# Attention forward and backward: queries repeated through DRAM, and o and dQ of a block taken from PSUM by one operation

## The chip, the cores and the metric

One core of one Trainium2 chip. The metric is the device time of one execution, in microseconds (us); for a set of runs the median is given. The engines are TensorE (PE, with its weight loads as PEld), VectorE (DVE), ScalarE (ACT) and GpSimd (POOL). SyncE (SP) issues DMAs and computes nothing. Each engine executes its instructions strictly in the order in which they were put into its queue.

## What is computed

The reference is the forward pass of two attention branches and its vector-Jacobian product with `grad_out`; it returns the joined output [1, 2048, 896] and the eight gradients (of both inputs and all weights). S = 2048, D = 448, 16 heads of 28 columns, bf16. Branch A is linear attention. Branch B, which the change touches, is softmax attention in which 16 query heads share one key head and one value head:

```python
q = (x @ wq).reshape(B, S, H, Dh).transpose(0, 2, 1, 3)
k = x @ wk
v = x @ wv
scores = jnp.einsum("bhqd,bkd->bhqk", q, k) * (Dh ** -0.5)
p = softmax(scores)
o = jnp.einsum("bhqk,bkd->bhqd", p, v)
return o.transpose(0, 2, 1, 3).reshape(B, S, H * Dh) @ wo
...
_out, _vjp = jax.vjp(_f, A_x, A_wqkv, A_wo, B_x, B_wq, B_wk, B_wv, B_wo)
_grads = _vjp(grad_out)
return (_out, *_grads)
```

## The kernel before

The program has three parts. Branch A, forward and backward, and the preparation of branch B take some 207 us. The main loop (L922) does the softmax attention forward and backward together, up to about 1000 us. A last part multiplies the gradients of queries, keys and values with weights and inputs.

**Units and blocks.** The loop runs `for u in range(NU + 28)`, NU = 512. A block b (64 of them, `blk(b)`) is 256 queries (`qc`, 8 of these) of two heads (`pair`); the 16 heads lie in four groups of four (g = pair // 2), 32 rows each, so that a block occupies 64 of a group's 128 rows (hp = pair % 2). A unit is two 128-row tiles of keys for the two heads of one block; eight units make a block. "u≡5" below is a unit with u mod 8 = 5. Everything inside the loop stands under `manual_schedule`: the order of each engine's queue is the order of the code.

**What one unit u issues.** PE multiplies queries and keys to scores S of unit u into two of three PSUM banks SB, and do and values to the gradient D of unit w = u − 16 into two banks DB (`rows_SD`, all recorded under L676). ACT exponentiates half 0 (L955) into eT, copies half 1 of D to SBUF (cp, L971) and exponentiates half 1 (L997): three activations of 128x512 a unit. DVE multiplies half 0 of D by eT into dsT (L967); POOL does half 1 from cp (L972). DVE then transposes dsT of unit u − 18 in 32x32 pieces into dsx (L1041). On even units PE accumulates `o_dq`: o of the units u − 2, u − 1 (from eT) in rows 0 to 63 of one PSUM bank `oq`, and dQ of the units u − 20, u − 19 (from dsT) in rows 64 to 127. On odd units it accumulates dK (`dk_m`) from dsx and qX, beginning with block b at u = 8b + 27.

**Once in four units** SP issues a DMA transpose of eT into eN (L999), which PE uses for dV 20 units after the block began.

**Once per block**, in this order: u≡1, DVE copies o from `oq` to the f32 tile oTs, rows 0 to 63 (L983); u≡2, PE transposes it into the spare SB bank (L809), DVE copies that back into oTs (L817), POOL multiplies it with do (L821), then the reciprocal of the row sums and two more POOL products (L830, L831); u≡3, DVE scales dQ of the block 19 units back out of `oq`, rows 64 to 127, into qT_B, over the queries of that block (L986); u≡4, `row_D`, a DVE sum (L835) and two short POOL products (L836, L837); u≡6, PE transposes the normalised gradient (L845) into the spare bank and DVE copies it to doT (L852). The spare bank is the bank into which the next unit's scores go, so that copy stands before them. `due(u, lag)` returns the block b for which u = 8b + lag.

**The queries for dK** lie in qX in another layout: four copies of each 32-row head piece, one for each quarter of the rows. For each `qc` and group, POOL copies the queries four times over into the one staging tile qst, in two operations of 128x512 (`qc_copy`, L856), and SP transposes it into qX (`qc_T`, L860, 128x1024). In every 64 units this is done in the units with u mod 64 = 29, 30, 37, 38, 45, 46, 53, 54, for the next 256 queries. The first 256 queries are done ahead of the loop by POOL and DVE. qX has two buffers, one for even and one for odd `qc`, each [128, 4, 2, 512].

**Beside these**, the attention's output products go to DRAM: from u = 144 a part of a row tile every 8 units, with a DVE copy (L747) and for each row tile one store on POOL's DMA queue (L749, 112 KB).

Of the kernel before, what the change touches and what calls it, by code (L numbers as in the profile page):

```python
# [9 lines left out]
ALU = mybir.AluOpType  # L10
AX = mybir.AxisListType
BF16 = mybir.dt.bfloat16
# [5 lines left out]
P = 128  # L18
# [7 lines left out]
def kernel(  # L26
# [624 lines left out]
    with ExitStack() as cs_:  # L651
        pe_ = cs_.enter_context(tc.tile_pool(name="ceT", bufs=1, side="right"))
        pn_ = cs_.enter_context(tc.tile_pool(name="ceN", bufs=1, side="right"))
        pd_ = cs_.enter_context(tc.tile_pool(name="cdsT", bufs=5, side="right"))
        pqa_ = cs_.enter_context(tc.tile_pool(name="cqXa", bufs=1, side="right"))
        px_ = cs_.enter_context(tc.tile_pool(name="cdsx", bufs=2, side="right"))
        pqb_ = cs_.enter_context(tc.tile_pool(name="cqXb", bufs=1, side="right"))
# [48 lines left out]

        woTp, gbT = R4, R2.rearrange("p t (c k) -> p t c k", k=P)

        qst = pp_.tile([P, 8, 4, 32], BF16, name="qst", bufs=1)[:, :, :, :]
        identF = pp_.tile([P, P], F32, name="identF", bufs=1)  # L710
        make_identity(nc, identF[:])
        oTs = pp_.tile([P, 256], F32, name="oTs", bufs=1)
        wo = pc_.tile([P, 4, D], BF16, name="wo", bufs=1)
        oTq = flat(R4).rearrange("p (t k) -> p t k", k=P)
        W4 = D // 4
# [97 lines left out]
        def o_copy(b):  # L813
            qc, pair, g, hp = blk(b)
            onp = onps.pop(b)
            os_ = oTs[:, 0:P].rearrange("p (q h c) -> p q h c", q=2, h=2)
# [34 lines left out]
            doT[b] = pw_.tile([P, 256], BF16, name="doT", bufs=2)  # L851
            nc.vector.tensor_copy(out=doT[b][r:r + 64, :], in_=tps2.pop(b)[r:r + 64, 0:256])  # L852

        def qc_copy(eng, st, qc, g, s):
            src = qT_B[g][:, qc * 256:(qc + 1) * 256].rearrange("p (b j s) -> p b j s", b=4, s=2)[:, :, :, s]
            eng.tensor_copy(out=st.rearrange("p (b s) a j -> p b s a j", s=2)[:, :, s, :, :],  # L856
                            in_=src.unsqueeze(2).to_broadcast([P, 4, 4, 32]))

        def qc_T(st, qc, g):
            nc.sync.dma_start_transpose(qX[qc].rearrange("p b s c -> p (b s) c")[:, :, g * P:(g + 1) * P],  # L860
                                        st.rearrange("p n a j -> p (n a j)"))

        dk_two = SB[2]

        def dk_m(b, m, other=0):
            qc, pair, g, hp = blk(b)
            h, B, s = m // 8, (m // 2) % 4, m % 2
            for a in range(4):
                rhs = dsx[b][32 * a:32 * a + 32, :, h, :, :].rearrange(
                    "p u t (b i s) -> p u t b i s", b=4, s=2)[:, :, :, B, :, s]  # L870
                k = 32 * ((a + 2) % 4) if other else 32 * a
                mmt((dk_two if other else dk_acc)[k:k + 32, :],
                    qX[qc][32 * a:32 * a + 32, B, s, pair * 64 + 32 * h:pair * 64 + 32 * h + 32],
                    rhs, (32 * a, k), other == 2 or b == 0 and m == 0, other == 0 and b == NB - 1 and m == 15)

        def o_mm(v):
            b, tp = divmod(v, 8)
# [43 lines left out]
        do_slots.update({32 + 8 * n: (13 + n // 4, n % 4 * P, n % 4 * P + P) for n in range(12)})  # L921
        with tc.manual_schedule():  # L922
            nc.sync.dma_start(wo, wo_d[:, 0:D].rearrange("(g p) c -> p g c", p=P))
            qX[0] = pqa_.tile([P, 4, 2, 512], BF16, name="qX")
            for g in range(4):
                st = pd_.tile([P, 2, 512], BF16, name="dsT").rearrange("p a (n j) -> p a n j", j=32).rearrange(
                    "p a (n b) j -> p (a n) b j", b=4)
                qc_copy(nc.gpsimd, st, 0, g, 0)
                qc_copy(nc.vector, st, 0, g, 1)
                qc_T(st, 0, g)  # L930
            for u in range(NU + 28):
                w = u - 16
                hasS = u < NU
# [29 lines left out]
                if hasD:  # L963
                    dst = pd_.tile([P, 2, 512], BF16, name="dsT")
                    dsT[w] = dst
                    ew = eT(w)
                    nc.vector.tensor_tensor(out=dst[:, 0, :], in0=dp[0][:, :], in1=ew[:, 0, :], op=ALU.mult)  # L967
                    if (b := due(u, 12)) is not None:
# [3 lines left out]
                    nc.gpsimd.tensor_tensor(out=dst[:, 1, :], in0=cp[:, :], in1=ew[:, 1, :], op=ALU.mult)  # L972
                gq, iq = divmod(u % 64 - 29, 8)
                qq = u // 64 + 1
                if 0 <= gq < 4 and u < 448:
                    if gq == 0 and iq == 0:
                        qX[qq] = (pqb_ if qq % 2 else pqa_).tile([P, 4, 2, 512], BF16, name="qX")
                    if iq < 2:
                        qc_copy(nc.gpsimd, qst, qq, gq, iq)
                if u == 7:  # L980
                    nc.vector.memset(oTs[64:128, :], 0.0)
# [14 lines left out]
                if hasS:  # L996
                    nc.scalar.activation(out=eT(u)[:, 1, :], in_=sp[1][:, :], func=ACT.Exp, scale=scale)  # L997
                    if u % 4 == 3:
                        nc.sync.dma_start_transpose(ENs[u // 4 % 6][:, :, :],  # L999
                                                    ETs[u // 4 % 5][:, :, :, :].rearrange("p a b c -> p (a b c)"))  # L1000
                    if 0 <= gq < 4 and iq == 1 and u < 448:
                        qc_T(qst, qq, gq)
# [157 lines left out]
```

## Time and profile before

| | |
|---|---|
| three runs | 1046.53, 1037.56, 1041.17 us; median 1041.17 |
| the profiled execution | 1044.09 us |
| its span | 1042.4 us, granted TensorE clock 1.0 |
| busy: PE, DVE, ACT, POOL | 1003.5 (96%), 886.9 (85%), 865.2 (83%), 812.3 (78%) us |
| L972, POOL product, 128x512 | x512, 584.6 us, 1156 ns each |
| L1041, DVE transpose, 128x512 f32 | x512, 356.7 us, 697 ns each |
| L967, DVE product, 128x512 | x512, 340.3 us, 665 ns each |
| L955, L997, L971, ACT, 128x512 | x512 each, 325.5, 333.4, 327.0 us |
| L856, POOL copy of queries, 128x512 | x56, 34.2 us, 611 ns each |
| L983, DVE o copy; L986, DVE dQ; 64x256 | x64 each, 405 and 427 ns |
| L852, DVE doT copy, 64x256 | x64, 288 ns |

How to read it: instructions on ACT and DVE overlap at their ends (ACT's activations last 0.64 us and start 0.48 us apart), so a sum of durations exceeds what an engine's time line holds; the busy time of a stretch counts covered time once. A row names the engine, the line, the operation, output <- input by the program's names, and the tile. "x4" after a time-line row means that four such instructions in a row were drawn as one. The DMA share is the mean over the 16 DMA engines that all queues use; packets in several queues count several times, so it can exceed 1.

### The profile page before, as it was taken

Reading aid. Unit: us, or ns where it says so; the run is one execution under the profiler, and the core shown is the slowest. Engines: PE = TensorE matmul, PEld = TensorE weight load, DVE = VectorE, ACT = ScalarE, POOL = GpSimd, SP = SyncE. Lnnn points to the kernel's source line nnn. Section 1 sums busy time; section 2 is a strip of 40 time slices with the busy share of each in tenths; the row PEclk is TensorE's granted clock in tenths of the full one; section 3 lists DMA queues with packets and bytes.
Section 4 is the critical chain, followed back from the end, with each engine's and each line's share of the span. In section 5 each row is a group of like instructions: output and inputs, shape, how many; then the busy total and the mean of one; then the engine's idle time right before and its main releaser. Section 6 shows DMA issues by size and latency. Waiting matters only on the chain.

```text
span 1042.4 us, 40109 instructions
## 1 busy us (share of the span) xinstructions
PE 1003.5 (96%) x16245; PEld 485.1 (47%) x16245; DVE 886.9 (85%) x1780; ACT 865.2 (83%) x1743; POOL 812.3 (78%) x1106
## 2 busy tenths in 40 slices
PE   9999999999999999999999999999999999999998
PEld 5555554434444444444444444444444444444444
DVE  7897500669999999999999999999999999999942
ACT  6463132599999999999999999999999999999632
POOL 8601282238998998999999989998999999889860
PEclk9999999999999999999999999999999999999999
DMA  9879999299999999999999999999999999999983
GB/s 261 157 137 191 176 229 218 38 161 201 194 187 192 187 193 194 202 187 194 201 193 195 192 187 204 198 182 202 188 197 186 195 195 195 200 188 203 228 168 90
DMA packets 689058, 195.15 MB, mean 187 GB/s; under 512 B 670408, under 2 KB 686688, under 8 KB 688872
## 3 DMA queue, kind: packets, MB, share of 16 engines
q1 hardware_dynamic: 680392, 179.97, 105.0%
q0 software_dynamic: 4544, 9.46, 3.0%
q10 hardware_dynamic: 3936, 3.16, 1.0%
q8 instruction: 127, 2.08, 0.8%
q14 instruction: 59, 0.48, 0.2%
HBM read 12.60 MB, written 10.84 MB: 22 GB/s over the span
## 4 chain that ended last, share of the span: by engine, by line
PE 39%; DVE 25%; POOL 16%; ACT 8%; issue 7%; DMA 3%; DVEq 0%; SPq 0%; ACTq 0%; POOLq 0%
PE agen L81 13%; POOL dsT L972 12%; DVE dsT L967 10%; PE agen L676 9%; DVE dsx L1041 9%; PE aacc L676 8%; PE aacc L81 7%; ACT cp L971 4%; ACT eT L997 2%; DMA eN<-eT 2%; DVE doT L852 1%; DVE R L986 1%; POOL qst L856 1%; POOL prod L821 1%; PE aacc L809 1%
## 5 line engine op out<-in xcount | busy, mean ns | idle before, releaser
L972 POOL TENSOR_TENSOR dsT<-cp,eT 128x512 bf16<-128x512 bf16 x512 | 584.6, 1156 | 49.4 <-ACT cp L971 42.6
L1041 DVE STREAM_TRANSPOSE dsx<-dsT 128x512 f32<-128x512 f32 x512 | 356.7, 697 | 5.8 <-POOL dsT L972 3.2
L676 PEld LDWEIGHTS <-R 32*128 32x128 bf16 (+1 forms) x9104 | 245.1, 94 | 243.3 <-issue 192.5
L967 DVE TENSOR_TENSOR dsT<-agen,eT 128x512 bf16<-128x512 f32 x512 | 340.3, 665 | 11.3 <-PE agen L676 5.4
L971 ACT ACTIVATE cp<-agen 128x512 bf16<-128x512 f32 x512 | 327.0, 639 | 11.8 <-PE agen L676 9.7
L955 ACT ACTIVATE eT<-aacc 128x512 bf16<-128x512 f32 x512 | 325.5, 636 | 12.0 <-PE agen L676 6.8
L997 ACT ACTIVATE eT<-aacc 128x512 bf16<-128x512 f32 x512 | 333.4, 651 | 0.0
L676 PE MATMUL agen<-dsx,qX 32*32 32x512 bf16 x4024 | 264.0, 376 | 0.0
L676 PE MATMUL agen<-doT,R 32*128 32x256 bf16 x2048 | 243.5, 269 | 4.1 <-DVE dsT L967 3.2
L676 PE MATMUL aacc<-R,R 32*128 32x256 bf16 (+1 forms) x2240 | 207.9, 267 | 16.7 <-DVE doT L852 6.6
L676 PE MATMUL agen<-dsT,R 128*32 128x256 bf16 x2048 | 155.5, 273 | 0.5 <-issue 0.5
L676 PE MATMUL agen<-eT,R 128*32 128x256 bf16 x2048 | 155.5, 273 | 0.1
L676 PEld LDWEIGHTS <-qX 32*32 32x32 bf16 x4096 | 78.3, 89 | 112.5 <-issue 54.1
L676 PE MATMUL aacc<-eN,don 128*32 128x512 bf16 x1024 | 91.7, 387 | 1.0 <-DMA eN<-eT 1.0
L81 PEld LDWEIGHTS <-R 128*128 128x128 bf16 x517 | 40.9, 98 | 41.0 <-issue 10.6
L81 PE MATMUL agen<-R,R 128*128 128x448 bf16 (+1 forms) x180 | 42.1, 361 | 0.3 <-DVE pq L244 0.3
L676 PEld LDWEIGHTS <-don 128*32 128x32 bf16 x1024 | 21.1, 93 | 42.5 <-issue 42.5
L856 POOL COPY qst<-R 128x512 bf16<-128x512 bf16 x56 | 34.2, 611 | 5.0 <-DVE dsx L1041 2.5
L821 POOL TENSOR_TENSOR prod<-R,oTs 128x128 f32<-128x128 bf16 x64 | 27.5, 430 | 9.0 <-DVE oTs L817 9.0
L586 DVE TENSOR_TENSOR osb<-R 32x512 bf16<-32x512 bf16 x4 | 1.7, 413 | 35.4 <-DMA R<-xa 33.8
L427 POOL COPY pk<-R 128x256 bf16<-128x256 bf16 x4 | 1.6, 399 | 37.7 <-DVE R L389 37.7
L262 POOL TENSOR_SCALAR wdq<-wdq 128x448 bf16<-128x448 bf16 x16 | 21.1, 1326 | 12.0 <-DVE phiT L243 12.0
(235 smaller groups left out, 1000.1 us busy)
## 6 DMA issues: line engine op xcount, KB each, us to landing
eN<-eT SPq DMA_TRANSPOSE x128
xa<-in_A_x_dram SPq DMA_DIRECT2D x8, 224.0 KB
ga<-in_grad_out_dram SPq DMA_DIRECT2D x4, 448.0 KB
out_dram<-osb ACTq DMA_DIRECT2D x16, 112.0 KB
xa<-in_grad_out_dram POOLq DMA_DIRECT2D x4, 448.0 KB, 7.1
out_dram<-wdq POOLq DMA_DIRECT2D x8, 224.0 KB, 5.5
eT<-in_grad_out_dram SPq DMA_DIRECT2D x4, 448.0 KB
eT<-in_B_x_dram SPq DMA_DIRECT2D x4, 448.0 KB
```

The costliest lines, as they stand in the source:

```text
L81: nc.tensor.matmul(out_ap, lhsT=lhsT, rhs=rhs, start=start, stop=stop, tile_position=(0, 0))
L262: nc.gpsimd.tensor_scalar(out=wq_n[:, st, 0:D], in0=wq_n[:, st, 0:D], scalar1=1.0, scalar2=None, op0=ALU.min)
L676: nc.tensor.matmul(out, lhsT=lhsT, rhs=rhs, start=start, stop=stop, tile_position=pos, skip_group_check=True)
L809: nc.tensor.transpose(onp[:, qb, :, :].rearrange("p h c -> p (h c)"), oTs[0:64, qb * P:(qb + 1) * P], identF[0:64, 0:64], tile_position=(0 ...
L821: nc.gpsimd.tensor_tensor(out=prod[b][:], in0=dnv, in1=os_, op=ALU.mult)
L856: eng.tensor_copy(out=st.rearrange("p (b s) a j -> p b s a j", s=2)[:, :, s, :, :], in_=src.unsqueeze(2).to_broadcast([P, 4, 4, 32]))
L955: nc.scalar.activation(out=eT(u)[:, 0, :], in_=sp[0][:, :], func=ACT.Exp, scale=scale)
L967: nc.vector.tensor_tensor(out=dst[:, 0, :], in0=dp[0][:, :], in1=ew[:, 0, :], op=ALU.mult)
L971: nc.scalar.activation(out=cp[:, :], in_=dp[1][:, :], func=ACT.Copy)
L972: nc.gpsimd.tensor_tensor(out=dst[:, 1, :], in0=cp[:, :], in1=ew[:, 1, :], op=ALU.mult)
L997: nc.scalar.activation(out=eT(u)[:, 1, :], in_=sp[1][:, :], func=ACT.Exp, scale=scale)
L1041: nc.vector.transpose(out=dsx[b][:, tp, :, :, :].rearrange("p h t c -> p (h t c)").bitcast(F32), in_=dsT[y][:, :, :].rearrange("p h c -> p ...
```

## The change

1. **Queries.** They are handled by group G of two blocks (32 groups of 16 units) and not by 256 queries of all groups. At u = 16G + 5 POOL makes one copy of 128x256 in another order of columns (`q_split`) and SP transposes it into a tile qtr. At u = 16G + 14 a DMA on POOL's queue writes qtr to DRAM four times (`q_out`, 512 rows of 512 bytes). At u = 16G + 20 another DMA on POOL's queue reads it back into qX (`q_in`, 128 rows of 2 KB), for `dk_m` from u = 16G + 27. qX is a pool of two buffers of [128, 4, 2, 128]. The 56 POOL copies and 28 transposes in the loop go, and so do the four POOL copies, four DVE copies and four transposes ahead of it.
2. **dQ.** Its products come 6 units later: units u − 26, u − 25 at an even u. From u = 514 on the rest is caught up, four units at a time. The pool of dsT grows from 5 to 11 buffers.
3. **o and dQ.** At u≡1 one DVE operation takes all 128 rows of `oq`, o of block b and dQ of block b − 3, into oTs, times a column that holds 1 in rows 0 to 63 and the scale in the others. At u≡5 DVE copies dQ from oTs to qT_B (SBUF to SBUF, f32 to bf16, 64x256). The first three o and the last three dQ are taken alone. The transposed o (L817) goes to a tile of its own, osu.
4. `row_D` of block 0, which was left out because no D is issued in that unit, runs at u = 12, and the memset of oTs is replaced by two of the scale column.

```diff
-        pd_ = ... tc.tile_pool(name="cdsT", bufs=5, side="right")
-        pqa_ = ... tc.tile_pool(name="cqXa", bufs=1, side="right")
-        pqb_ = ... tc.tile_pool(name="cqXb", bufs=1, side="right")
+        pd_ = ... tc.tile_pool(name="cdsT", bufs=11, side="right")
+        pq_ = ... tc.tile_pool(name="cqX", bufs=2, side="right")
...
-        qst = pp_.tile([P, 8, 4, 32], BF16, name="qst", bufs=1)[:, :, :, :]
+        qst = pp_.tile([P, 2, 32, 4], BF16, name="qst", bufs=1)[:, :, :, :]
+        qtr = pp_.tile([P, 2, P], BF16, name="qtr", bufs=1)[:, :, :]
+        q_d = [dpool.tile([512, 256], BF16, name=f"q_d{i}") for i in range(32)]
...
+        osu = pp_.tile([P, P], F32, name="osu", bufs=1)
+        o_dq_scale = pp_.tile([P, 1], F32, name="odqs", bufs=1)
+        dqs = {u: (u - 26, u - 25) for u in range(0, NU + 1, 2)}
+        dqs.update({NU + 2 + 2 * n: tuple(range(488 + 4 * n, 492 + 4 * n)) for n in range(4)})
+        dqs.update({NU + 12 + 2 * n: (504 + 2 * n, 505 + 2 * n) for n in range(4)})
...
-        def qc_copy(eng, st, qc, g, s):
-            src = qT_B[g][:, qc * 256:(qc + 1) * 256].rearrange("p (b j s) -> p b j s", b=4, s=2)[:, :, :, s]
-            eng.tensor_copy(out=st.rearrange("p (b s) a j -> p b s a j", s=2)[:, :, s, :, :],
-                            in_=src.unsqueeze(2).to_broadcast([P, 4, 4, 32]))
-
-        def qc_T(st, qc, g):
-            nc.sync.dma_start_transpose(qX[qc].rearrange("p b s c -> p (b s) c")[:, :, g * P:(g + 1) * P],
-                                        st.rearrange("p n a j -> p (n a j)"))
+        def q_split(G):
+            qc, g = divmod(G, 4)
+            src = qT_B[g][:, qc * 256:(qc + 1) * 256].rearrange("p (b j s) -> p s j b", b=4, s=2)
+            nc.gpsimd.tensor_copy(out=qst, in_=src)
+            nc.sync.dma_start_transpose(qtr, qst.rearrange("p s j b -> p (s j b)"))
+
+        def q_out(G):
+            nc.gpsimd.dma_start(q_d[G].rearrange("(a p) c -> p a c", a=4),
+                                qtr.rearrange("p s c -> p (s c)").unsqueeze(1).to_broadcast([P, 4, 256]))
+
+        def q_in(G):
+            qX[G] = pq_.tile([P, 4, 2, P], BF16, name="qX")
+            nc.gpsimd.dma_start(qX[G].rearrange("p b s c -> p (b s c)"), q_d[G].rearrange("(p b) c -> p (b c)", b=4))
...
+        def dq_to(b):
+            qc, pair, g, hp = blk(b)
+            return qT_B[g][64 * hp:64 * hp + 64, qc * 256:(qc + 1) * 256]
...
-                if 0 <= gq < 4 and u < 448:
-                    if gq == 0 and iq == 0:
-                        qX[qq] = (pqb_ if qq % 2 else pqa_).tile([P, 4, 2, 512], BF16, name="qX")
-                    if iq < 2:
-                        qc_copy(nc.gpsimd, qst, qq, gq, iq)
+                if u == 12:
+                    row_D(0)
+                if hasS and u % 16 == 5:
+                    q_split(u // 16)
+                if hasS and u % 16 == 14:
+                    q_out(u // 16)
+                if 0 <= u - 20 < NU and u % 16 == 4:
+                    q_in(u // 16 - 1)
...
                 if (b := due(u, 9)) is not None:
-                    nc.vector.tensor_copy(out=oTs[0:64, :], in_=oq[0:64, 0:256])
-                if (b := due(u, 27)) is not None:
-                    qc, pair, g, hp = blk(b)
-                    nc.vector.tensor_scalar(out=qT_B[g][64 * hp:64 * hp + 64, qc * 256:(qc + 1) * 256],
-                                            in0=oq[64:128, 0:256], scalar1=scale, scalar2=None, op0=ALU.mult)
+                    if b < 3:
+                        nc.vector.tensor_copy(out=oTs[0:64, :], in_=oq[0:64, 0:256])
+                    else:
+                        nc.vector.tensor_scalar(out=oTs[:, :], in0=oq[:, 0:256], scalar1=o_dq_scale[:, 0:1], scalar2=None,
+                                                op0=ALU.mult)
+                if (b := due(u, 37)) is not None and b < 61:
+                    nc.vector.tensor_copy(out=dq_to(b), in_=oTs[64:128, :])
...
                 else:
-                    o_dq((u - 2, u - 1), (u - 20, u - 19))
+                    ys = dqs.get(u, ())
+                    o_dq((u - 2, u - 1), ys[:2])
+                    o_dq((-1, -1), ys[2:])
```

The new copy at u≡5 is called "the cast L999" in the prediction, after its line in the changed kernel.

More of the change, by code (lines that the diff above doesn't have):

```diff
@@ L653 @@
         pn_ = cs_.enter_context(tc.tile_pool(name="ceN", bufs=1, side="right"))
-        pd_ = cs_.enter_context(tc.tile_pool(name="cdsT", bufs=5, side="right"))
-        pqa_ = cs_.enter_context(tc.tile_pool(name="cqXa", bufs=1, side="right"))
+        pd_ = cs_.enter_context(tc.tile_pool(name="cdsT", bufs=11, side="right"))
+        pq_ = cs_.enter_context(tc.tile_pool(name="cqX", bufs=2, side="right"))
         px_ = cs_.enter_context(tc.tile_pool(name="cdsx", bufs=2, side="right"))
-        pqb_ = cs_.enter_context(tc.tile_pool(name="cqXb", bufs=1, side="right"))
         pc_ = cs_.enter_context(tc.tile_pool(name="ccp", bufs=3, side="right"))
@@ L815, in o_copy @@
             onp = onps.pop(b)
-            os_ = oTs[:, 0:P].rearrange("p (q h c) -> p q h c", q=2, h=2)
+            os_ = osu[:, :].rearrange("p (q h c) -> p q h c", q=2, h=2)
             nc.vector.tensor_copy(out=os_, in_=onp)
@@ L872, in dk_m @@
                 mmt((dk_two if other else dk_acc)[k:k + 32, :],
-                    qX[qc][32 * a:32 * a + 32, B, s, pair * 64 + 32 * h:pair * 64 + 32 * h + 32],
+                    qX[b // 2][32 * a:32 * a + 32, B, s, hp * 64 + 32 * h:hp * 64 + 32 * h + 32],
                     rhs, (32 * a, k), other == 2 or b == 0 and m == 0, other == 0 and b == NB - 1 and m == 15)
+        def dq_to(b):
+            qc, pair, g, hp = blk(b)
+            return qT_B[g][64 * hp:64 * hp + 64, qc * 256:(qc + 1) * 256]
         def o_mm(v):
@@ L923 @@
             nc.sync.dma_start(wo, wo_d[:, 0:D].rearrange("(g p) c -> p g c", p=P))
[L924 to L930, printed above, removed]
             for u in range(NU + 28):
@@ L967 @@
                     nc.vector.tensor_tensor(out=dst[:, 0, :], in0=dp[0][:, :], in1=ew[:, 0, :], op=ALU.mult)
-                    if (b := due(u, 12)) is not None:
+                    if u > 12 and (b := due(u, 12)) is not None:
                         row_D(b)
@@ L972 @@
                     nc.gpsimd.tensor_tensor(out=dst[:, 1, :], in0=cp[:, :], in1=ew[:, 1, :], op=ALU.mult)
-                gq, iq = divmod(u % 64 - 29, 8)
-                qq = u // 64 + 1
-                if 0 <= gq < 4 and u < 448:
-                    if gq == 0 and iq == 0:
-                        qX[qq] = (pqb_ if qq % 2 else pqa_).tile([P, 4, 2, 512], BF16, name="qX")
-                    if iq < 2:
-                        qc_copy(nc.gpsimd, qst, qq, gq, iq)
+                if u == 12:
[6 more added lines that the diff above has]
+                    q_in(u // 16 - 1)
                 if u == 7:
-                    nc.vector.memset(oTs[64:128, :], 0.0)
+                    nc.vector.memset(o_dq_scale[0:64, :], 1.0)
+                    nc.vector.memset(o_dq_scale[64:128, :], scale)
                 if (b := due(u, 9)) is not None:
-                    nc.vector.tensor_copy(out=oTs[0:64, :], in_=oq[0:64, 0:256])
-                if (b := due(u, 27)) is not None:
-                    qc, pair, g, hp = blk(b)
-                    nc.vector.tensor_scalar(out=qT_B[g][64 * hp:64 * hp + 64, qc * 256:(qc + 1) * 256],
-                                            in0=oq[64:128, 0:256], scalar1=scale, scalar2=None, op0=ALU.mult)
+                    if b < 3:
[5 more added lines that the diff above has]
+                    nc.vector.tensor_copy(out=dq_to(b), in_=oTs[64:128, :])
+                if u in (517, 521, 531):
+                    b = {517: 61, 521: 62, 531: 63}[u]
+                    nc.vector.tensor_scalar(out=dq_to(b), in0=oq[64:128, 0:256], scalar1=scale, scalar2=None, op0=ALU.mult)
                 if (b := due(u, 10)) is not None:
@@ L1000 @@
                                                     ETs[u // 4 % 5][:, :, :, :].rearrange("p a b c -> p (a b c)"))
-                    if 0 <= gq < 4 and iq == 1 and u < 448:
-                        qc_T(qst, qq, gq)
                 if u % 2:
```

## The prediction, made before the changed kernel was run

> **What bounds the kernel now.** I read the chain of waits first, then the busy time by stage, then one ordinary block in the timeline, then the lines that the change touches. The profiled execution took 1044.09 us, its span 1042.4, so 1.7 lie around it; the median of the three runs is 1041.17. The sum is made on 1044.1, 2.9 above that median, and the number I give is half way between the two bases (1042.6 plus the sum). At the runs' scatter, 1037.6 to 1046.5, about 1% is what a measurement of this kernel can tell from no change.
>
> ```profile
> PE 39%; DVE 25%; POOL 16%; ACT 8%; issue 7%; DMA 3%; DVEq 0%; SPq 0%; ACTq 0%; POOLq 0%
> ```
>
> No engine owns the chain: it changes engine every few instructions. So look at the main loop alone (core busy time in a stretch):
>
> ```profile
> 252.50:441.50 189.00, 184.06 (x3648) 87.20 (x3643) 185.50 (x367) 188.88 (x384) 176.52 (x224) 1.00 1.20 193
> 958.00:1042.40 84.40, 76.34 (x920) 36.14 (x915) 47.78 (x88) 36.87 (x71) 47.12 (x65) 1.00 0.81 166
> ```
>
> The columns after the length are PE, weight load, DVE, ACT, POOL, clock and DMA. In the loop's first long stretch ACT is covered for 188.88 of 189.00 us, DVE 185.50, PE 184.06, POOL 176.52. The five loop stretches to 958 us look alike: over 705.5 us DVE idles 18.0 and POOL 47.9. What can be saved there is small; what can be lost is anything that adds to DVE or POOL beyond their idle time, or delays one of them at a step for which the others wait. The copy of the first block's o (L817) starts at 219.4, the last at 973.9, so a block of 8 units takes (973.9 − 219.4)/63 = 11.98 us; ordinary blocks take 11.77 to 11.84. ACT issues three activations a unit, 24 a block. Their closest spacing in ordinary stretches is 0.477 us, which gives 11.45; with the longer slot that a unit has once, 1.447 a unit, 11.58. The rest of a block is in the units with an extra step, above all u≡5 and 6 (mod 8; 1.53 us each), where DVE is late:
>
> ```profile
> 604.38 0.65 DVE L967 TENSOR_TENSOR dsT<-agen,eT 128x512 bf16<-128x512 f32 x1
> 604.96 0.69 DVE L1041 STREAM_TRANSPOSE dsx<-dsT 128x512 f32<-128x512 f32 x1
> 605.58 0.65 DVE L967 TENSOR_TENSOR dsT<-agen,eT 128x512 bf16<-128x512 f32 x1
> 606.26 0.29 DVE L852 COPY doT<-aacc 64x256 bf16<-64x256 bf16 x1
> ...
> 606.43 0.70 ACT L997 ACTIVATE eT<-aacc 128x512 bf16<-128x512 f32 x1
> 607.01 0.61 ACT L955 ACTIVATE eT<-aacc 128x512 bf16<-128x512 f32 x1
> ...
> 604.57 0.22 POOL L837 TENSOR_TENSOR don<-Dq,rl 128x4 bf16<-128x4 f32 x1
> 604.72 4.63 POOL L972 TENSOR_TENSOR dsT<-cp,eT 128x512 bf16<-128x512 bf16 x4
> ...
>   PE aacc L676: 6.6, 30
> ```
>
> DVE runs back to back from L967 to the doT copy (L852). Only that copy frees the bank for the next unit's scores; the last line (who waits for L852) shows PE doing so 30 times, and ACT's next step comes 0.58 us after its last one and not 0.48. So the time from u≡5 to L852 on DVE is on the path.
>
> **The change part by part.** *Queries, POOL.* Removed: 56 copies at 0.61 us, 34.2 us. Added, 32 times: a 128x256 copy (0.40, row L427), an issue over 512 rows and one over 128. The nearest issues are L94, 512 rows at 0.76, and L749, 128 rows at 0.58. 32 × (0.40 + 0.76 + 0.58) = 55.7; less 34.2, and 3.2 for what starts the loop, about +18 us. POOL has 47.9 idle, so this fits, but POOL ends near 96%, and an issue ahead of a product (L972) delays it by its length; the wait ends on DVE's transpose L1041 one or two units later, which is the slack. I take nothing, with +2 us as upper end.
>
> *Queries, what was waited for.* POOL's copies into the single staging tile waited for the queued transpose of the one before:
>
> ```profile
>   POOL qst L856: 2.5, 4
> ...
> L860 SPq DMA_TRANSPOSE qX<-qst x28: 1235/1264/2050, 256.0 to 868.8; - x28
> L999 SPq DMA_TRANSPOSE eN<-eT x128: 4832/5440/6272, 213.8 to 971.0; - x128
> ```
>
> With the 2.5 us in which POOL waited for DVE before the same copies, that is 5.0, and the blocks that hold them are the long ones (12.5 to 13.0 us). Now a staging tile is refilled 16 units later, when its transpose has long run: −5. At the loop's start four copies each on POOL and DVE and four transposes go: −1.
>
> *Queries, DMA.* The queue on SP is never empty: eN transposes follow each other every 5.5 us, 4 to 11 us behind ACT. It loses 32 transposes of 1.26 us (40 us) and gets 32 of a quarter of the bytes, estimated at 0.4 from that row (13 us), while 16.8 MB of plain traffic arrive:
>
> ```profile
> q1 hardware_dynamic: 680392, 179.97, 105.0%
> q0 software_dynamic: 4544, 9.46, 3.0%
> ```
>
> The first row is 105% × 1042.4 / 179.97 = 6.08 us of 16 engines per MB, the second 3.3. 6.3 MB fewer transposed is −38 us, 16.8 MB more plain +55: net +17 us over 755, about 2% of queue time. eN is wanted 11 us after ACT, so I cost this at nothing in the loop while that cover holds. In the last 8 blocks the old kernel moved no queries and the lag fell to 1 us; now a load goes in at unit 516, and the load behind the last eN transpose comes later: +1.5 (0 to 5).
>
> *o and dQ.* Per block DVE loses two PSUM copies (L983 0.405, L986 0.427) and gets one of 128x256, taken at 0.427, since a row's time goes with columns, and an SBUF-to-SBUF cast of 64x256 (L999), 0.28 by L852 (64x256, 0.288). Sum: −0.12 us, not in u≡3 but with the new cast in u≡5, right between L967 and L1041 of the timeline above. Had it to pay for itself only, 61 × −0.12 = −7 off the path: worth 0 to −2. But POOL begins a product of 1.16 us at 604.72, and the cast would come at 604.8 to 605.0. Only at two places does the trace show a DVE operation of one SBUF source and an SBUF target beside POOL:
>
> ```profile
> L627 DVE TENSOR_SCALAR gaT<-gaT x3: 414/414/416, 193.3 to 202.6; 16x512 int32<-16x512 int32 x3
> ...
> L627 DVE TENSOR_SCALAR dsT<-dsT x1: 821/821/821, 210.2 to 210.2; 16x512 int32<-16x512 int32 x1
> ...
> 208.44 2.29 POOL L856 COPY dsT<-R 128x512 bf16<-128x512 bf16 x3
> ...
> 21.96 1.32 POOL L262 TENSOR_SCALAR wdq<-wdq 128x448 bf16<-128x448 bf16 x1 [0.62 <-DVE phiT L243]
> 22.50 0.28 DVE L243 TENSOR_SCALAR phiT<-osb 128x448 bf16<-128x448 bf16 x1
> ```
>
> L627 took 0.821 us beside POOL's copies and 0.414 alone: held 0.41. L243, 0.54 us into a POOL operation, was not held (others of its row, started together with POOL's, took 0.63 to 0.70). So the hold lies between 0 and what is left of the product, 605.88 − 605.0 = 0.87. I take 0.41, as the cast comes early in POOL's operation like L627, less the 0.15 that DVE is ahead after losing L986: +0.25 on the path, × 61 = +15. Longer holds would give (0.87 − 0.12) × 61 = +46.
>
> *The rest.* Products of dQ move from u to u+6 on PE, same number; eleven dsT buffers cover the longer life. The joint PSUM copy waits for PE's last o product as L983 did, and the dQ products before it in the same unit, so no wait is new. Row sum 0, run now and not before, is three operations of 0.2 us once. The catch-up units after 512 hold more products, where PE is busy 76.3 of 84.4 us already; the products are the same, so 0, at most +2.
>
> Sum: −5 − 1 + 1.5 + 15 = +10.5; 1054.6 on the profiled execution, 1051.7 on the median, and I say 1053.
>
> The Trainium skill, "SBUF — State Buffer", section "Who interferes with whom", says that DVE's copies and casts within SBUF can take a port pair shared with GpSimd and that whoever issues first keeps it for the whole instruction. L627 agrees in kind (0.41 of holding), L243 at 22.50, unheld within POOL's operation, does not. By the rule the sum would be that of the second rival.
>
> **Rivals.** *Not held, or the cast comes before the product:* for it speaks L243; against it L627 and the start times. Then −5 − 1 + 1.5 and 0 to −2 for DVE: 1036 to 1038. *Held for all that is left of the product:* +46 in place of +15, 1084; for it speaks that L627's end, 211.00, fits its waiting for the third POOL copy, which ended at 210.73; against it L243. *Faster by over 1%:* with DVE relieved at u≡3 and POOL's stalls gone, blocks fall to ACT's 11.58 to 11.6: (11.96 − 11.60) × 60 = −22, 1021; it decides if the cast costs under 0.1 us and the waits at u≡6 vanish. Against it: L852 still waits for the same chain. *DMA becomes the bound:* the new traffic costs the queue more than it saves, and the lag grows. q_out waits for the small transpose, which lands about the lag plus 9.3 us after ACT's last step of its units, while POOL comes to q_out 17.2 us after it; beyond a lag of 7.9 POOL stands, with L972 queued behind and L1041 waiting. At 2 us each, every second time, 16 × 2 = 32 on top of −4.5 from the other terms: 1070. Lags of 4 to 11 today speak for it, the slack of DMA time at the loop's end against.
>
> **How the numbers follow.** Forecast 0.42; not held 0.25; held for all 0.13; DMA 0.12; faster blocks 0.08. Against the median 1041.2, over 1051.6 lie some two thirds of the forecast's cases and both slow rivals; under 1030.8 only the faster blocks and a little of "not held". So faster 0.12, same 0.36, slower 0.52. The forecast's own range, hold 0.3 to 0.6, is 1046 to 1064 (hold less 0.15, × 61, less 4.5). For 8 in 10: low end 1031, short of the faster blocks; high end 1077, between the DMA rival and the full hold.
>
> **What would show it.** In the new trace the cast L999 lasts about 0.7 us where it starts within 0.4 us of a POOL product, and L852 and ACT's next step come 0.2 to 0.3 later in that block; blocks 22, 23, 37, 38 and 54 are ordinary; POOL waits for no DMA. The prediction is wrong if L999 shows 0.28 us throughout (then about 1037), if POOL waits at the two new DMA issues, or if the end of the loop grows by over 5 us.

## The result, and the profile after

The changed kernel takes 1097.74 us (median of four, 1096.0 to 1099.05); the kernel before took 1040.63 (four, 1037.56 to 1046.53). The ratio is 1.054, 95% interval 1.049 to 1.059: 5.4% slower, outside the forecast range of 1031 to 1077. The profiled execution took 1096.0 us, span 1094.3, against 1044.09 and 1042.4: +51.9. Ratios below leave out runs that took over 1.5% longer than the fastest run of the same kernel (two of e2's four, one each of e3's and e6's), and the trace of e3 is of such a run.

All of it is in the loop. The first copy of the transposed o now starts at 219.3 us and the last at 1025.9, 806.6 apart for 754.5 before: +52.1, or 12.80 us a block for 11.98. What lies ahead of it and behind it is as long as before.

The chain of waits of the changed kernel by engine:

```profile
PE 43%; DVE 33%; POOL 7%; issue 7%; ACT 7%; DMA 3%; DVEq 0%; ACTq 0%; POOLq 0%
```

and the busy time of one stretch of the loop, before and after (length, then PE, weight load, DVE, ACT, POOL, clock, DMA share, GB/s):

```profile
441.50:630.50 189.00, 183.43 (x3642) 87.12 (x3640) 184.75 (x366) 187.57 (x382) 177.49 (x228) 1.00 1.20 193
441.50:630.50 189.00, 170.25 (x3398) 79.55 (x3401) 185.85 (x342) 175.96 (x357) 172.60 (x221) 1.00 1.12 193
```

DVE has moved up in the chain from 25 to 33%, and in the stretch it is the only engine still covered as before (185.85 of 189, 184.75 there before). ACT fell from 187.57 to 175.96, PE from 183.43 to 170.25 and POOL from 177.49 to 172.60, and PE issued 3398 instructions where it had issued 3642. The others wait for DVE, and DVE is busy with something that is not work. The timeline of DVE, POOL and ACT around one cast (start, length):

```profile
603.95 0.69 DVE L975 TENSOR_TENSOR dsT<-agen,eT 128x512 bf16<-128x512 f32 x1
604.67 1.21 DVE L999 CAST R<-oTs 64x256 bf16<-64x256 f32 x1
605.92 0.71 DVE L1056 STREAM_TRANSPOSE dsx<-dsT 128x512 f32<-128x512 f32 x1
606.55 0.65 DVE L975 TENSOR_TENSOR dsT<-agen,eT 128x512 bf16<-128x512 f32 x1
607.23 0.29 DVE L858 COPY doT<-aacc 64x256 bf16<-64x256 bf16 x1
...
604.58 3.42 POOL L980 TENSOR_TENSOR dsT<-cp,eT 128x512 bf16<-128x512 bf16 x3
...
606.30 0.70 ACT L1012 ACTIVATE eT<-aacc 128x512 bf16<-128x512 f32 x1
607.99 0.60 ACT L963 ACTIVATE eT<-aacc 128x512 bf16<-128x512 f32 x1 [0.98 <-PE agen L675]
```

POOL starts three products at 604.58, 1.14 us each, so the first ends at about 605.73. The cast starts 0.09 us into it and ends at 605.88, 0.15 after it, having taken 1.21 us for 0.29 of work. Behind it come L1056, L975 and the doT copy L858, which PE needs for the next scores; ACT's next step comes 1.69 us after its last instead of the 0.58 at this place before. This repeats in nearly every block. The row of the cast (minimum, median and maximum in ns):

```profile
L999 DVE CAST R<-oTs x61: 291/1208/1227, 260.3 to 1030.4; 64x256 bf16<-64x256 f32 x61
```

and the view of waits, who waited for whom (us in all, times, longest):

```profile
PE aacc L675 <- DVE doT L858: 66.6, 62, 1.2
```

Of the 61 casts, 60 start within a product of POOL, and each of these ends 0.15 or 0.16 us after that product does, whether it came 0.1 or 0.85 us into it. The one that came beside a short POOL operation took 0.29 us. PE's wait for the doT copy grew from 6.6 us in 30 waits to 66.6 in 62.

The mean time from one unit's first exponential to the next unit's, by u mod 8, over units 64 to 503 of each trace, shows where a kernel's blocks are long. The rows below the first two belong to the experiments.

| kernel | 0 | 1 | 2 | 3 | 4 | 5 | 6 | 7 |
|---|---|---|---|---|---|---|---|---|
| before | 1.511 | 1.477 | 1.546 | 1.447 | 1.487 | 1.529 | 1.525 | 1.446 |
| changed | 1.499 | 1.446 | 1.568 | 1.489 | 1.431 | 1.434 | **2.514** | 1.447 |
| e4, before + a cast | 1.501 | 1.446 | 1.499 | 1.447 | 1.451 | 1.532 | **2.513** | 1.447 |
| e7, dQ and o alone | 1.499 | 1.446 | 1.568 | 1.447 | 1.430 | 1.435 | **2.563** | 1.447 |
| e8, cast at u≡4 | 1.500 | 1.446 | 1.571 | 1.447 | 1.430 | **2.085** | 1.537 | 1.447 |
| e2, two PSUM copies | 1.558 | 1.451 | **2.153** | 1.541 | 1.444 | 1.435 | 1.477 | 1.489 |
| e10, sum at u≡7 | **1.846** | 1.454 | 1.556 | 1.447 | 1.430 | 1.434 | 1.485 | 1.472 |
| e12, ACT at u≡2 | 1.546 | 1.448 | **1.906** | 1.430 | 1.430 | 1.440 | 1.482 | 1.453 |
| e1, queries alone | 1.538 | 1.447 | 1.588 | **1.908** | **2.072** | 1.530 | 1.488 | 1.442 |
| e14, traffic alone | 1.546 | 1.447 | 1.499 | 1.447 | **2.343** | 1.523 | 1.467 | 1.440 |

In the changed kernel the slot of u≡6 costs 0.99 us more and the other seven together 0.13 less: +0.86 a block. In e4, which has none of the change's savings, it is 0.99 more and 0.12 less.

DMA, of the changed kernel: the eN transposes, the small one of the queries, and the two new DMAs' issues on POOL:

```profile
L1014 SPq DMA_TRANSPOSE eN<-eT x128: 4777/5342/6954, 211.7 to 1022.1; - x128
...
L864 SPq DMA_TRANSPOSE qtr<-qst x32: 1167/1169/1791, 216.7 to 1007.6; - x32
...
L867 POOL DMA_DIRECT2D q_d<-qtr x32: 798/798/847, 222.5 to 1020.5; - x32
...
L872 POOL DMA_DIRECT2D qX<-q_d x32: 582/583/598, 235.8 to 1030.6; - x32
```

(The duration of a transpose is that of SP's instruction; the trace has no landing time for it.) The eN transposes are no slower than before (5.34 us, 5.44 before), and they now start on average 1.2 us after the last exponential that they need, not 6.7; this is called the lag. Read from this profile alone, the new way of the queries looks free. The experiments say otherwise.

### The profile page after: what moved, and what is told of

It reads as the page before. It is cut to its first block, busy times and chain, and to the rows that moved or that the text cites. A ratio compares the mean times of both kernels' runs of the same rounds, so it can differ in the third digit from the quotient of the medians.

```text
span 1094.3 us, 39601 instructions
## 1 busy us (share of the span) xinstructions
PE 999.4 (91%) x16245; PEld 478.9 (44%) x16245; DVE 937.8 (86%) x1778; ACT 869.7 (79%) x1743; POOL 842.5 (77%) x1144
## 3 DMA queue, kind: packets, MB, share of 16 engines
q0 software_dynamic: 9664, 26.24, 8.7%
## 4 chain that ended last, share of the span: by engine, by line
PE 43%; DVE 33%; POOL 7%; issue 7%; ACT 7%; DMA 3%; DVEq 0%; ACTq 0%; POOLq 0%
PE agen L81 13%; DVE dsT L975 13%; PE agen L675 12%; PE aacc L675 10%; DVE dsx L1056 9%; PE aacc L81 6%; POOL dsT L980 6%; DVE R L999 5%; ACT cp L979 3%; DMA qX<-q_d 2%; ACT eT L1012 2%; DVE oTs L996 1%; DVE doT L858 1%; DVE osu L823 1%; ACT eT L963 1%
## 5 line engine op out<-in xcount | busy, mean ns | idle before, releaser
L980 POOL TENSOR_TENSOR dsT<-cp,eT 128x512 bf16<-128x512 bf16 x512 | 588.8, 1158 | 73.2 <-ACT cp L979 69.7
L675 PEld LDWEIGHTS <-R 32*128 32x128 bf16 (+1 forms) x9104 | 238.4, 94 | 300.3 <-issue 243.7
L1056 DVE STREAM_TRANSPOSE dsx<-dsT 128x512 f32<-128x512 f32 x512 | 358.5, 700 | 3.1
L975 DVE TENSOR_TENSOR dsT<-agen,eT 128x512 bf16<-128x512 f32 x512 | 343.6, 671 | 11.5 <-PE agen L675 8.2
L675 PE MATMUL aacc<-R,R 32*128 32x256 bf16 (+1 forms) x2240 | 207.6, 267 | 73.8 <-DVE doT L858 66.6
L675 PE MATMUL agen<-doT,R 32*128 32x256 bf16 x2048 | 256.2, 270 | 2.7 <-DVE dsT L975 1.9
L999 DVE CAST R<-oTs 64x256 bf16<-64x256 f32 x61 | 68.6, 1125 | 1.9
L827 POOL TENSOR_TENSOR prod<-R,osu 128x128 f32<-128x128 bf16 x64 | 27.5, 430 | 11.8 <-DVE osu L823 11.8
L262 POOL TENSOR_SCALAR wdq<-wdq 128x448 bf16<-128x448 bf16 x16 | 21.1, 1327 | 12.1 <-DVE phiT L243 12.1
```

The lines of the kernel that those rows point to most:

```text
L262: nc.gpsimd.tensor_scalar(out=wq_n[:, st, 0:D], in0=wq_n[:, st, 0:D], scalar1=1.0, scalar2=None, op0=ALU.min)
L675: nc.tensor.matmul(out, lhsT=lhsT, rhs=rhs, start=start, stop=stop, tile_position=pos, skip_group_check=True)
L999: nc.vector.tensor_copy(out=dq_to(b), in_=oTs[64:128, :])
L1056: nc.vector.transpose(out=dsx[b][:, tp, :, :, :].rearrange("p h t c -> p (h t c)").bitcast(F32), in_=dsT[y][:, :, :].rearrange("p h c -> p ...
```

## The experiments

Times are medians; ratios are to the kernel before, run on the same chip beside each set (1042 to 1044 us).

### First set: the cast, and each half by itself

**e4: the cast in the kernel before.** Everything else is as before; the values written (into rows of doT that nobody reads) are used by no one. It ran in 61 blocks, not 57.

```diff
+                if (b := due(u, 37)) is not None and b < 61:
+                    jb = u // 8 - 2
+                    jr = 64 * (jb % 2)
+                    nc.vector.tensor_copy(out=doT[jb][jr:jr + 64, :], in_=oTs[64:128, :])
```

> The kernel before plus one copy of 64x256 f32 to bf16 from SBUF to SBUF on DVE at u≡5 of 57 blocks (into rows of doT that nobody reads); everything else as before. Theory: each is held to about 1.2 us, and a block takes 0.9 to 1.0 longer, 1092 to 1100 us. Rival (the copy only costs its own time): 57 x 0.28 = 16, 1057.

Measured: 1097.65 us, 1.051 (1.050 to 1.053). The cast alone makes the changed kernel's loss, in the same unit (2.513 in the table). Its row (busy us, mean ns):

```profile
L991 DVE CAST doT<-oTs 64x256 bf16<-64x256 f32 x61 | 50.7, 831 | 1.9
```

**e3: the same step as another operation.** In the changed kernel the cast becomes a sum over one element each, with the same tile, place and values.

```diff
-                    nc.vector.tensor_copy(out=dq_to(b), in_=oTs[64:128, :])
+                        nc.vector.tensor_reduce(out=dq_to(b), in_=oTs[64:128, :].unsqueeze(2), axis=AX.X, op=ALU.add)
```

> The changed kernel, with the copy at u≡5 written as a sum over one element each: same place, tile, source, target and values, another DVE operation. Theory, if the waiting belongs to the copy alone: 0.3 to 0.4 us each, never held, 1038 to 1050 us. If any DVE operation from SBUF to SBUF waits for POOL's product there: 1.2 us each and 1095 or more.

Measured: 1100.25 us, 1.052 (1.048 to 1.056), so the time was missed widely, but for another reason than either theory's. The step itself was as the theory had it. Its row shows that it is never held:

```profile
L1000 DVE TENSOR_REDUCE R<-oTs x61: 414/416/417, 260.9 to 1041.6; 64x256 bf16<-64x256 f32 x61
```

The view of waits shows PE waiting for eN and qX instead, which it did for 0 and 2.4 us in the changed kernel:

```profile
PE aacc L675 <- DMA eN<-eT: 17.3, 17, 3.6
...
PE agen L675 <- DMA qX<-q_d: 9.8, 12, 1.9
```

With the hold gone, DMA is what PE waits for most, beside the 23.8 us that are left of the wait for the doT copy. Many blocks are 12.0 us, some are 15 to 18.

**e2: no cast.** o and dQ are taken from PSUM by two operations at u≡1.

```diff
-                        nc.vector.tensor_scalar(out=oTs[:, :], in0=oq[:, 0:256], scalar1=o_dq_scale[:, 0:1], ...)
-                if (b := due(u, 37)) is not None and b < 61:
-                    nc.vector.tensor_copy(out=dq_to(b), in_=oTs[64:128, :])
+                    nc.vector.tensor_copy(out=oTs[0:64, :], in_=oq[0:64, 0:256])
+                if (b := due(u, 33)) is not None and b < 61:
+                    nc.vector.tensor_scalar(out=dq_to(b), in0=oq[64:128, 0:256], scalar1=scale, ...)
```

> The changed kernel, but o and dQ are taken from PSUM at u≡1 by two DVE operations, dQ straight into its place; no cast at u≡5. Theory: u≡6 falls from 2.5 to about 1.5 us, 1034 to 1042 us in all. Rival (DVE is simply too full at this place, whatever the operation): DVE has more to do than in the changed kernel (0.83 us a block for 0.77), only its place differs, so at most some 15 us are won, 1080.

Measured: 1102.12 us, 1.047 (1.039 to 1.055); its runs spread from 1086.6 to 1112.3. The theory missed the time: u≡6 fell to 1.48 as expected, but u≡2 rose to 2.15. The dQ operation now stands on DVE ahead of the copy of the transposed o, for which PE waits (view of waits):

```profile
PE aacc L675 <- DVE osu L823: 39.6, 61, 1.0
```

and PE waits for qX as well. So this run removed one cost and put another in its place.

**e1: the queries alone.** The kernel before with `q_split`, `q_out`, `q_in` and the small qX, o and dQ as before.

> The kernel before with the new way of the queries alone (split, DRAM, read back); dQ and o are taken as before. Theory (the lost time is the cast at u≡5, which waits for POOL's product to end): this part costs nothing and saves what POOL waited for, so 1032 to 1040 us against some 1041 before. Rival (the time went to POOL's new DMA issues and to the plain DMA traffic): most of the +57 us shows here, 1075 or more.

Measured: 1108.44 us, 1.059 (1.054 to 1.063). The theory, which had this half at nothing, fell. The row of its eN transposes, and then its waits:

```profile
L997 SPq DMA_TRANSPOSE eN<-eT x128: 4858/5798/8889, 212.5 to 1037.2; - x128
```

```profile
PE aacc L675 <- DMA eN<-eT: 21.0, 17, 2.6
...
PE agen L675 <- DMA qX<-q_d: 16.3, 15, 2.6
...
POOL q_d L862 <- DMA qtr<-qst: 7.5, 6, 2.4
```

The eN transposes now take 5.80 us in the middle and 8.9 at most, and lag 8.5 us on average; dV waits for eN, dK for qX, and POOL for qtr. The lost time is in the units where dV and dK begin (u≡3 and 4 in the table), in some blocks and not in others. Behind the loop another 10 us are lost (78.4 us from the last copy of the transposed o to the end, 68.5 before): PE waits 8.2 us there for a load that stands behind the late transposes on SP's queue.

### Second set: dQ's half without the queries, and the traffic

**e7: dQ and o alone.** The changed kernel with the queries copied by POOL and transposed as before, per group of 16 units.

```diff
-                if hasS and u % 16 == 5:
-                    q_split(u // 16)
-                if hasS and u % 16 == 14:
-                    q_out(u // 16)
-                if 0 <= u - 20 < NU and u % 16 == 4:
-                    q_in(u // 16 - 1)
+                if hasS and u % 16 in (13, 14):
+                    qc_copy(u // 16, u % 16 - 13)
...
+                    if u % 16 == 14:
+                        qc_T(u // 16)
```

> The changed kernel with queries copied and transposed as before (two POOL copies and one 128x1024 transpose for every 16 units, straight into the small qX; one output staging tile instead of two): the part of dQ and o alone. Theory: the held cast alone makes the loop's length, 1090 to 1100 us, as in the changed kernel. If the two parts add up instead: well under 1097, 1060 or less.

Measured: 1097.46 us, 1.052 (1.051 to 1.054), as expected. Each half alone costs 5 to 6%, and both together 5.4%.

**e8: e7 with the cast at u≡4**, behind the sum L841.

> As the run before, with the cast one unit earlier, behind the sum L841 at u≡4, where POOL waits for that sum and runs short products. Theory: the cast comes before POOL's next product or is held 0.2 us at most, no DMA stall, 1034 to 1046 us. If the place does not matter: 1090 to 1100.

Measured: 1074.99 us, 1.031 (1.029 to 1.032), between the two. The cast came 0.3 us into the product that POOL was still on, and was held there too; its row:

```profile
L973 DVE CAST R<-oTs 64x256 bf16<-64x256 f32 x61 | 59.3, 973 | 1.9
```

It takes 0.97 us (the row above: busy us in all, mean ns), and 0.65 of it shows in u≡5 (2.09, where the changed kernel has 1.43).

**e5: plain traffic in the kernel before**, two writes of 256 KB in every 16 units on POOL's queue, which nothing waits for.

```diff
+                if hasS and u % 16 == 14:
+                    nc.gpsimd.dma_start(q_d[u // 16].rearrange("(a p) c -> p a c", a=4),
+                                        wo[:, 0, 0:256].unsqueeze(1).to_broadcast([P, 4, 256]))
+                if hasS and u % 16 == 4:
...
```

> The kernel before plus two plain writes of 256 KB (512 rows of 512 bytes) from a constant tile to DRAM in every 16 units, issued on POOL's queue where the change issues its two; nothing waits for them, queries and dQ as before. Theory (the plain traffic takes the 16 DMA engines from the eN transposes): eN transposes take 5.8 to 6.0 us instead of 5.4, dV waits for eN, 1080 to 1110 us. Rival (what costs is that dK waits for queries that arrive late through DRAM): no wait here, 1041 to 1048.

Measured: 1112.29 us, 1.066 (1.065 to 1.068). eN takes 5.89 us, PE waits 21.7 us for it and POOL 16.4 us for the queries' transposes. That is as the theory has it, with the time a little above its range, but this run adds 51 us of POOL time too, so it doesn't separate the two.

**e6: the same issues with 4 bytes a row.**

> As the run with the plain traffic, the same 64 issues with the same 512 rows each, but 4 bytes a row instead of 512. Theory: hardly any bytes, eN as before, 1041 to 1052 us. Rival (POOL's time for the issues, some 32 x 2 x 0.8 = 51 us, is what costs): the same time as with 512 bytes a row.

Measured: 1332.61 us, 1.273 (1.270 to 1.276). Neither. With 0.13 MB instead of 16.8, the transposes suffer far more (one eN transpose took 16.8 us, the mean is 7.6 for 5.9 in e5); why is not shown, and the run says nothing on POOL's time.

### Third and fourth sets: which of traffic, POOL's time and latency it is, and a faster version

**e9: the kernel before with its queries per 16 units** (as in e7), the base of the next two.

> The kernel before with its queries handled by 16 units and not by 64: the same two POOL copies of 128x512 and one 128x1024 transpose for each group of two blocks, evenly spread, into a small qX; nothing ahead of the loop; dQ and o as before. Theory (the long blocks 22, 37, 54 and the others come from copies that wait for the queued transpose of the copy 8 units before): they become ordinary, 1034 to 1041 us against some 1043. If the lag of SP's queue only falls elsewhere: 1042 to 1048.

Measured: 1049.41 us, 1.006 (1.005 to 1.008), above both ranges. The copies' long blocks 22, 37 and 54 went, but eN's lag grew in the later blocks (8.6 us over the last eight, 5.3 before), with some of 12.4 to 13.1 there. The loop, from the first to the last copy of the transposed o, is 753.3 us, 1.2 less than before. The time is lost behind it (74.1 us for 68.5): SP's queue reaches the loads of the last part late, PE waits for one (view of waits), and its clock is at half for 6.8 us there.

```profile
PE aacc L81 <- DMA eT<-in_grad_out_dram: 4.7, 1, 4.7
```

**e13: POOL's time alone**, e9 plus two memsets.

```diff
+                if hasS and u % 16 in (4, 14):
+                    nc.gpsimd.memset(junk, 0.0)
```

> The kernel before with queries by 16 units (as e9_group, 1049 us) plus two POOL memsets of some 0.8 us in every 16 units, where the change issues its two DMAs: POOL's time for the issues without their traffic. Theory (the traffic is what costs in e5_traffic): +0 to +10 on e9_group, 1047 to 1060 us. Rival (POOL's time is what costs): 1095 or more.

Measured: 1052.95 us, 1.010 (1.008 to 1.012), 3.5 above e9; the memsets took 54.1 us in all. They cost 9 us in the loop (762.6 for 753.3), and 6 come back behind it (68.3 for 74.1), where the queue lags less (2.8 us over the last eight blocks). So 54 us more of POOL work cost 4 to 9 us.

**e14: the traffic without POOL**, e9 plus the writes of e5, issued by ACT.

> As e9_group plus the same two plain writes of 256 KB in every 16 units as in e5_traffic, issued from ACT's queue: the traffic without POOL's time. Theory: eN transposes take 5.8 to 6.0 us, PE waits for eN, 1085 to 1115 us. Rival (POOL's time): as e9_group, 1050, plus a few us for ACT's issues.

Measured: 1096.84 us, 1.052 (1.050 to 1.054), 47 above e9. The eN transposes take 5.65 us in the middle (5.44 in e9), a little less than expected. The time is in u≡4 (2.34), where dV begins. u≡6, where half of the writes are issued, is as short as ever (1.47), so ACT's own issues are not what costs. The chain of waits by engine and line, and then PE's wait for eN (3.3 us in e9):

```profile
PE 44%; DMA 31%; DVE 14%; ACT 5%; issue 4%; POOL 2%; SPq 0%; DVEq 0%; POOLq 0%; ACTq 0%
DMA eN<-eT 30%; PE agen L675 13%; PE agen L81 13%; PE aacc L675 10%; DVE dsT L962 6%; PE aacc L81 6%; DVE dsx L1037 5%; ACT cp L966 2%; ACT eT L993 1%; POOL dsT L967 1%; DVE R L982 1%; PE aacc L810 1%; DVE doT L853 1%; DVE Dq L836 0%; PE agen L313 0%
```

```profile
PE aacc L675 <- DMA eN<-eT: 34.4, 32, 2.7
```

**e15: the queries alone, each step 8 units earlier**, three buffers of qX.

> The new way of the queries alone (as e1_q_only, 1108 us) with each step 8 units earlier and three buffers of qX, so that the same DMAs have 12 us more to land. Theory (DMA engine time): PE no longer waits for qX, but eN stays as slow (5.8 to 6.0 us) and PE waits for it, 1070 to 1105 us. Rival (only the round trip's latency costs): 1036 to 1046.

Measured: 1102.52 us, 1.059 (1.055 to 1.063). PE no longer waits for qX, and waits for eN for 37.2 us instead of 21.0 (view of waits):

```profile
PE aacc L675 <- DMA eN<-eT: 37.2, 25, 4.5
```

So the latency of the round trip isn't the cause: with it hidden, the wait for eN remains, and the time with it.

**e11: q_out writes once, q_in repeats while it reads.**

```diff
-            nc.gpsimd.dma_start(q_d[G].rearrange("(a p) c -> p a c", a=4),
-                                qtr.rearrange("p s c -> p (s c)").unsqueeze(1).to_broadcast([P, 4, 256]))
+            nc.gpsimd.dma_start(q_d[G], qtr.rearrange("p s c -> p (s c)"))
...
+                                q_d[G].rearrange("(j b) c -> j (b c)", b=4).unsqueeze(0).to_broadcast([4, 32, 1024]))
```

> The new way of the queries alone (as in e1_q_only), but q_out writes qtr to DRAM once (64 KB) and q_in repeats it while reading (256 KB): 0.33 MB in 16 units for 0.52. Theory (DMA engine time): eN transposes take 5.6 to 5.8 us, the time lies between the kernel before and e1_q_only, 1055 to 1090 us. If the number of issues or the round trip's latency is what costs: as e1_q_only, 1100 or more.

Measured: 1129.77 us, 1.084 (1.081 to 1.086), slower than e1 with fewer bytes. The eN transposes' median fell to 5.60, as expected, but the read is made of more packets (14272 on that queue for 9664), lands 9.0 us after its issue instead of 7.7, and PE waits 42.8 us for qX and its weight loads 50.0. Byte count alone does not price a DMA.

**e10 and e12: dQ's half without a held cast.** e7 with the one-element sum at u≡7, and e7 with the copy made by ACT at u≡2.

> The part of dQ and o alone (queries by POOL copies and transposes as in e7_old_q), with the copy of dQ as a one-element sum on DVE, at u≡7, behind the doT copy. Theory: never held and not ahead of L852, so u≡6 and u≡7 stay at 1.45 to 1.5 us, 1034 to 1045 us. If DVE is full there: 0.3 us a block more, 1055.

> The part of dQ and o alone (as e7_old_q), with the copy of dQ made by ACT at u≡2. Theory: ACT is not held beside POOL's products and takes some 0.3 us; about 0.1 of it lies in ACT's wait at u≡2, so a block takes 11.9 to 12.0, 1040 to 1048 us. If ACT is held too: 1080 or more.

Measured: 1054.15 us, 1.011 (1.010 to 1.013), and 1056.04, 1.013 (1.012 to 1.015). Neither is held (0.416 and 0.414 us each). The sum costs 0.35 us in the unit behind it (u≡0 1.85, 1.50 in e7): the second alternative, DVE full there. The copy on ACT costs as much in its own unit (u≡2 1.91, 1.57 in e7).

**e16: e9 with no query transposes in the last 70 units.**

> As e9_group, but a group every 14 units with 7 buffers of qX, so that the last 70 units have no query transposes, as in the kernel before. If e9_group lost by SP's queue lagging in the last blocks: 1034 to 1042 us, as fast as the kernel before or faster. If not: 1046 to 1050 as e9_group.

Measured: 1048.46 us, 1.005 (1.003 to 1.007). The time is that of e9, but it lies elsewhere. eN's lag over the last eight blocks is down to 4.1 us, and behind the loop it takes 68.2 us, as before the change: e9's loss was the lag at the end. In the loop it takes 4.4 us longer than before (758.9): POOL waited 7.7 us for queued transposes, at four copies, and beside the longest of these waits (4.4 us) a block takes 16.3 us. No version here beats the kernel before.

## Why the prediction was wrong, step by step

**The hold was there, but its size was taken from the wrong end of its bounds.** The forecast named the cast L999, waiting for POOL's product between L967 and L1041, with the doT copy behind. All of that is what the trace shows, and e4 shows that it suffices. The failing step is "I take 0.41, as the cast comes early in POOL's operation like L627". The hold is not an amount but a time of release: the end of POOL's product, 0.15 us later for the cast (so for 243 of the 244 casts of the changed kernel, e4, e7 and e8, whose lengths run from 0.44 to 1.23 us). With a start 0.1 us into a product of 1.16 that is 0.92 (1.208 − 0.291). Two further terms were off. The cast's own 0.29 was booked against the PSUM copies that went, but those lay in u≡1 and 3 while the cast lies ahead of L858, so it is on the path too: 0.92 + 0.29 = 1.21 for the operation. And the lead of 0.15 that was subtracted is worth nothing here. DVE did come earlier, by 0.4 us against ACT, but a wait that ends with POOL's product takes that back: in e4, without the lead, the cast starts 0.49 us into the product and takes 0.81, and u≡6 grows by the same 0.99. In both kernels the transpose behind the cast starts 2.0 us after ACT's first exponential of u≡5, where it started at 1.0 before. So the path grew by 0.99 a block where the sum had 0.25. The rival "held for all that is left" (1084) had the mechanism, and lacked the cast's own time. None of the three signs of being wrong came up; what did not fit was the 0.7 us set for the cast.

The row that misled was L243, unheld within POOL's L262. The row that told the truth was L627, whose end fitted the end of the third POOL copy; the prediction said so under the rival and then gave it 0.13. "Only at two places does the trace show" such an operation was wrong too. Just ahead of L627 stand four DVE copies from SBUF to SBUF (minimum, median and maximum in ns):

```profile
L856 DVE COPY dsT<-R x4: 501/690/828, 207.8 to 209.4; 128x512 bf16<-128x512 bf16 x4
```

The two long ones (826 and 828) start 0.25 us into a copy of POOL's and end 0.28 us after it, as L627 does (0.27). With them the rows against L243 would have been three. The Trainium skill, "SBUF — State Buffer", section "Who interferes with whom", has the shared ports kept for the whole instruction, and a reduction as an operation that never contends. For POOL's products beside a cast (60 of 60 released at the end) and for the one-element sum (0.414 to 0.417 us, 61 of 61) these runs agree with both. The first does not fit L243: eight of these, started 0.49 to 0.62 us into an L262 of 1.32, took 0.27 to 0.28 us. Why they were not held was not tried.

**The queries' new way "at nothing in the loop while that cover holds".** In the changed kernel this held, but only because the cast had made the loop longer. Two terms were mis-sized. "32 of a quarter of the bytes, estimated at 0.4" took 1.17 us each, hardly less than the 1.26 of the whole ones, so SP's queue was spared 32 × 0.1 = 3 us and not 27. And the whole effect on the DMA engines was priced at +17 us: with the queries alone an eN transpose takes 5.89 us on average for 5.42 (e1), 128 × 0.47 = 60 us of that queue. Four eN transposes and the small one then take 4 × 5.89 + 1.19 = 24.8 us in every 16 units, where an ordinary stretch before lasts 2 × 11.8 = 23.6: the cover is gone. (e1's own 16 units last 26.0 us, so the queue alone is not the whole of it.) In the changed kernel, with the same traffic, an eN transpose takes 5.40 us on average; with the small one that is 22.8 us in 16 units of 25.6, and they fit. So two halves of 5 to 6% make 5.4% together, and taking the cast's hold away (e3) won nothing. The DMA rival, with 0.12 and 1070, had the growing lag right, but its path only in part: in e1 POOL stands 7.5 us at q_out, where it set 32, while PE waits 21.0 us for eN and 16.3 for qX. And it was written as an alternative to the hold, when it was a second bound behind it.

e13 to e15 settle which part of the DMAs costs: the traffic (+47 us), not POOL's issues (+3.5, in the loop +9) and not the latency. The clock has a small part. In the profiled run of e1 it is 0.978 on average against 1.0, and PE is busy 24 us longer for the same work (1027.3 for 1003.5). Its trace has ten stretches of 3.4 or 6.8 us in the loop at half the clock, 37 us in all, each begun 1 to 4 us after PE came to a stand of 1.2 to 2.6 us; the kernel before has none in its loop. An estimate from this: 37 us at half the clock lose at most 19 of the 64 us. That the waits lower the clock was not tried.

**What was right, and what only looks so.** POOL took the issues, and in the changed kernel its waits for queued transposes are gone. The products of dQ 6 units later cost nothing that e7's row would show. The end of the loop did not grow, where +1.5 was set, since the queue of transposes no longer lags; with the queries alone it grew by 10 us. The joint PSUM operation took 0.475 us, where 0.427 was set. The savings of −5 and −1 can't be read from the changed kernel: the other seven slots of its blocks are 0.13 us shorter, but those of e4, which has POOL's copies and their transposes as before, are shorter by 0.12. Behind the hold they were worth nothing, as the two kernels' times show (1097.74 and 1097.65); and in e9, without the cast, evenly spread copies shortened the loop by 1.2 us.

## What to carry to other kernels

Before putting a copy, a cast or a scaling from SBUF to SBUF on DVE, look at what POOL executes in that place: beside a long POOL product, price it at that product's remaining time plus its own, and count no lead of DVE against that; or read from PSUM (the 64 L986 took 0.425 to 0.428 us here), or use a form that isn't held. When a profile shows a part as free, ask whether another slow part pays for it: run that part alone, since two bounds behind one another show only the first. In a queue of DMA transposes with no slack, count plain traffic by what it adds to each transpose, and test it with traffic that nobody waits for.

## What the runs showed that was not expected

- A DMA transpose of 128x256 took 1.17 us, one of 128x1024 1.26 and one of 128x4096 5.4: the small one saves bytes, but no time.
- A queue of transposes that lags at the end of the loop delays the loads of the next part: with the queries alone that cost 10 us behind the loop, in e9 5.6.
- 64 DMAs with 512 rows of 4 bytes each lengthened the kernel by 290 us, where 512 bytes a row cost 69.
- On DVE, the one-element sum took 0.416 us where the cast needs 0.29, and was the cheaper of the two beside POOL's products (0.416 for 0.81 in e4 and 1.21 in the changed kernel).
- POOL's product in L262, a scaling in place of 1.32 us, did not hold L243 beyond about its first 0.4 us; the products L972 and L980 held the cast to their end.
